# A fused attention and MLP block on one core: first loads split, W1's and Wkv's tails as steps of their own, all steps in a new order

## The chip, the cores and the metric

The kernel runs on one core of a Trainium2 chip. Its engines are TensorE (PE, with its weight loads as PEld), VectorE (DVE), ScalarE (ACT), GpSimd (POOL) and SyncE (SP); SP and ACT also issue the DMA transfers here, each on a queue of its own. The metric is the device time in microseconds (us). Before the change it is 150.41 us, the median of 3 runs (150.39 to 150.41).

## What is computed

The reference, cut to its core (bf16 inputs; S = 2048 tokens, D = 448, H = 16 heads of 28, F = 1792):

```python
xn = layernorm(x)                       # over D, eps 1e-5
q, k, v = split_heads(xn @ wqkv)
pq, pk = q @ w_phi, k @ w_phi           # per head, 28 x 28
phi_q = concat(softmax(pq), softmax(-pq))
phi_k = concat(softmax(pk), softmax(-pk))
kv, z = phi_k^T @ v, sum(phi_k)         # over the tokens
o = (phi_q @ kv) / (phi_q @ z + 1e-6)
h = xn @ w1 + b1
out = x + merge_heads(o) @ wo + (h * tanh(softplus(h))) @ w2
```

## The kernel before

The 2048 tokens are 16 tiles of 128 tokens; tile t holds every sixteenth token. Two tiles, 2u and 2u+1, form pair u; there are 8 pairs. The weights of q and k are multiplied with w_phi first (Wpq, Wpk), so that PE computes pq and pk directly. D = 448 is three chunks of 128 rows and a tail of 64; each tail is loaded twice, into either half of the 128 partitions, and the matmuls of a pair run two at a time on halves of 64 rows.

The program is recorded as named steps, and the string `ORDER` (L147 to L160) gives the order in which they are recorded. An engine runs its instructions in that order, so the string sets the order on PE, DVE, ACT, POOL and on the two DMA queues alike; waits on semaphores are put in from the data that each step reads and writes (`Program.op`, `resolve`). The banks of PSUM are also given out in that order: a step that needs a pair of banks takes the one that was given back longest ago (`take2`), and waits for whatever still reads it.

The steps of which the prediction speaks (a last letter names the engine or queue: s SP, a ACT, d DVE, p POOL, m the transposing DMA on SP):

- `lx..`: load of tiles of x (L269). `lkm`, `lvm`: the 384 main rows of Wk, Wv (L272). `lkt`: the tails of Wk and Wv in one (they are neighbours in memory), two DMAs (L279). `l1m0` to `l1m2`, `l1t`: W1's three chunks and its two tails. `lqT0` to `lqT3`: Wq, transposed by the DMA (L284); `qd` then copies 64 rows inside it on DVE (L288). `lp`: w_phi. `lb`: b1.
- `st6d`: mean and variance of tile 6, two rows on DVE (L467, L468), or three on ACT (`st3a`, L459 to L463). `rs3`: one over the standard deviation of pair 3, on ACT (L480, L482) or POOL (L473, L476). `xn3`: the normalised pair 3, three rows on DVE (L501), or a small shift on DVE (L489) and three rows on POOL (L496).
- `xt3`: the transposed pair 3, by seven PE transposes (L509) and a copy out of PSUM (L514 or L516), or by a DMA (L521).
- `z12`: 12 matmuls on constants at the start (L376). `wtk0` to `wtk3`: a chunk of Wk transposed on PE (wtr, L556) and copied out; `wmk0`.., `wmq0`..: a chunk of Wpk or Wpq, four matmuls with w_phi (wmm, L571) and a copy out. `b1`: a transpose on PE and a copy.
- `v31`, `v32`, `k31`, `q31`: first part (8 matmuls) and second part (6) of v, pk and pq for pair 3, all on L438. The second part is followed by the copy (L514, L516) or by two exponentials on ACT (L600 for k, L661 for q).
- `kn3.0`: half of phi_k's normalisation for pair 3: two rows on DVE (L608, L610) and a scaling on POOL (L612). `kv3`: the pair's part of kv (L629). `kvz`: kv out of PSUM, and a DMA transpose. `e4`: DMA transpose of tile 4's exponentials of q (L669).
- `f0.11`: first part of ffn1 for 128 features and half of the tokens (L438, 512 columns; ACT's Mish at L680 follows the second). `nd4`: numerator and denominator of tile 4 (L703), and DVE's seven rows on them. `ot2`: transpose of pair 2's o. `wo`, `G`, `g`: the matmuls with Wo and W2 (L843, L821, L805) and, with the last of a tile, the add on DVE (L770). `sto`: store of a pair.

Pair 3 is the first pair to be worked on, then pair 1; both are transposed on PE. Pair 2 is the first one transposed by the DMA.

Of the kernel before, what the change touches and what calls it, by code (L numbers as in the profile page):

```python
# [144 lines left out]


ORDER = """  # L147
lpa pp2 lx3s pm z12 st6d pi lkms table st7d pw lx1a lkts lba lvma bd rs3t wtk2a xn3d lx2s lqT2 wtk0d st3d pv wtk1a wmk2a
xt3a wtk3d lqT1 wmk0a wmk1a st2d wmk3a st5d v31d rs1p lqT0 st4d xn1d rs2p lqT3 b1 qd lx6s v32a k31 lx0s wmq1a lx4s pp1
wmq0a xn2p l1ts xt1d st14d st15d wmq2a wmq3a k32 k11 st12d rs7p st9d q11 xt2m st8d k12 st10d xn7d q31 rs4p v11d pp0 q12  # L150
xn4p st11d v12d q21 rs5p st13d q32 q22 xn5p k21 st0d l1m2s l1m0s rs6p xt7m v21d k22 st1d v22a ep e3 rs0p v71a pk xt4m
k71 v72a kn3.1 xn6d k72 xt5m k41 xn0d kn3.0 e2 xt6m xt0m v41d e5 k42 l1m1s v42d e4 q41 v51d q42 e6 e8 v52a kn2.0 k61
v61d k62 kn4.0 k01 k51 kn7.0 kn4.1 k02 v62d q51 k52 q52 kn0.0 e7 q61 e9 v01d q62 e12 kn1.1 kn6.1 e10 f0.11 e11 kn1.0
v02d f0.12 kn0.1 f1.01 f0.21 f1.02 f1.21 kn7.1 f1.31 f1.22 los kn2.1 q71 f1.32 f1.51 kn5.0 f0.22 e13 f1.52 q01 q72 q02
f0.61 l2s kn6.0 kv3 kv1 e15 kv2 kn5.1 kv4 kv6 e14 kv7 kv0 kv5 kvz f0.62 f0.71 f0.91 f1.81 f0.72 e1 f1.82 f0.121 f1.111
f0.122 f0.81 f0.92 f1.112 f0.82 f1.91 f0.131 f1.92 e0 nd2 f0.132 f0.31 f0.101 f0.32 nd0 f0.111 f0.102 f0.112 nd1 f1.71
f1.61 f1.72 f0.51 nd3 f1.62 f0.52 f1.41 f1.11 f0.01 f1.12 f0.41 f1.42 ot0m nd5 f0.42 f0.02 wo01 f1.131 f1.101 ot1m nd6
f1.132 G01 nd4 f1.102 G11 ot2m wob nd7 ot3m G02 wo02 f1.121 nd12 G12 f1.122 wo11 nd11 wo22 G31 wo31 nd10 wo12 G21 nd13
ot5m ot6m wo21 wo32 G62 nd8 G22 wo52 G32 nd9 ot4m wo61 G51 nd15 G61 nd14 wo51 G41 wo62 sto6 sto1 wo41 G52 ot7m g14 sto5
wo7F sto2 G42 wo7H sto0 wo42 g15 stt14 sto3 sto4 stt15  # L160
"""


# [5 lines left out]
def _kernel(es, nc, A_x, A_wqkv, A_w_phi, A_wo, B_w1, B_b1, B_w2, out):  # L169
    def sb(name, shape, dtype):  # L170
        return es.enter_context(nc.sbuf_tensor(name, shape, dtype))

# [103 lines left out]
    def load_chunk(eng, name, dst, src, c):  # L276
        dma(eng, lambda e: e.dma_start(dst[:, c, :], src[c * P:(c + 1) * P, :]), w=[(name, 0, c)], tag=f"ld{name}.{c}")
# [272 lines left out]
    def w_tr(c, eng):  # L550
        b = take1()
        to = bank16(b)[0:GP, 0:G * P].rearrange("p (g n) -> p g n", g=G)

        def tr(e):
            for g in range(G):
                ins = e.transpose(to[:, g, :], Wk[:, c, g * GP:(g + 1) * GP], ident[:])  # L556
# [431 lines left out]
```

## Time and profile before

| | |
|---|---|
| time, 3 runs | 150.39 to 150.41 us, median 150.41 |
| the profiled execution's own time | 150.35 us |
| its span, from the first to the last instruction | 148.3 us |
| granted TensorE clock | 0.999 |
| PE busy | 143.7 us (97%) |
| DVE busy | 100.7 us (68%) |
| ACT busy | 72.0 us (49%) |
| POOL busy | 44.4 us (30%) |
| share of the chain that ended last | PE 89%, DMA 6%, DVE 2% |

The profile is of one execution. A row of the timeline gives the start in us from the span's start, the busy time of a group of instructions that follow each other, the engine (or SPq, ACTq for the issuing of DMAs), the line, the operation, what it writes and reads by the program's tile names, the number of instructions, and in brackets how long the engine sat idle before it and what ended that. A matmul's own duration overlaps that of the next one, so the price of a matmul is read from start to start. A row of the chain of work that ended last gives start, length and the work. A row of the DMA issues ends with the time from issue to landing (the median, if there are several). In the tile names, Eq is also the home of the transposed Wk, and W stands for W1 or W2.

### The profile page before, as it was taken

The numbers are of one execution on the slowest core, as the hardware profiler recorded it, in microseconds if no ns is written. First come the engines' busy times: TensorE is split into PE (matmuls) and PEld (weight loads), VectorE is DVE, ScalarE is ACT, GpSimd is POOL, SyncE is SP. The second block draws the span as 40 slices with busy tenths as digits, with TensorE's granted clock in tenths as the row PEclk, the third lists the DMA queues.
The fourth block names the chain that finished last, engine by engine and source line by source line (L and its number), as shares of the span: only waits on it lengthen the run. The fifth ranks groups of instructions, "written<-read, shape, count | busy, mean of one in ns | idle before, by whom it ended". The sixth has DMA issues, their size and how long they took to land.

```text
span 148.3 us, 3988 instructions
## 1 busy us (share of the span) xinstructions
PE 143.7 (97%) x1731; PEld 75.9 (51%) x1731; DVE 100.7 (68%) x225; ACT 72.0 (49%) x83; POOL 44.4 (30%) x65
## 2 busy tenths in 40 slices
PE   7799999999999999999999999999999999999993
PEld 2456456556555475444454445555555555554452
DVE  0888889897999803003998278896789859983042
ACT  3589889978996899578566653202000000000000
POOL 5428489899899990000000000000000000000000
PEclk9999999999999999999999999999999999999999
DMA  5999998999939989960003300031003300306513
GB/s 123 301 190 346 182 275 130 163 205 256 139 67 174 242 242 267 210 113 0 0 4 62 62 4 0 21 73 34 4 2 66 62 0 4 62 4 186 186 52 134
DMA packets 39997, 17.24 MB, mean 116 GB/s; under 512 B 33964, under 2 KB 39212, under 8 KB 39980
## 3 DMA queue, kind: packets, MB, share of 16 engines
q1 hardware_dynamic: 38800, 16.29, 52.5%
q10 hardware_dynamic: 1180, 0.70, 1.9%
q8 instruction: 13, 0.21, 0.6%
q14 instruction: 4, 0.03, 0.1%
HBM read 7.02 MB, written 1.84 MB: 60 GB/s over the span
## 4 chain that ended last, share of the span: by engine, by line
PE 89%; DMA 6%; DVE 2%; issue 0%; ACT 0%; SPq 0%
PE PS L438 47%; PE PS L843 31%; PE PS L805 3%; DMA Wkv<-in_A_wqkv_dram 3%; DMA xnT<-xn 3%; PE PS L703 2%; PE PS L629 2%; PE PS L571 1%; PE PS L821 1%; DVE stats L467 1%; PE PS L556 1%; PE PS L509 1%; DVE xnT L516 0%; ACT Eq L514 0%; DVE x_all L770 0%
## 5 line engine op out<-in xcount | busy, mean ns | idle before, releaser
L438 PE MATMUL PS<-xnT,W 64*128 64x512 bf16 x392 | 44.8, 376 | 0.0
L680 ACT ACTIVATE actT<-PS,b1T 128x1024 bf16<-128x1024 f32 x28 | 30.1, 1112 | 24.3 <-PE PS L438 24.3
L843 PE MATMUL PS<-W,actT 64*128 64x448 bf16 x392 | 39.3, 349 | 0.0
L438 PEld LDWEIGHTS PS<-xnT,W 64*128 64x128 bf16 x392 | 18.8, 94 | 20.8 <-ACT actT L680 0.5
L843 PEld LDWEIGHTS PS<-W,actT 64*128 64x128 bf16 x392 | 18.1, 94 | 18.1 <-issue 0.3
L612 POOL TENSOR_TENSOR actT<-actT,rSk 128x896 bf16<-128x896 bf16 x16 | 26.6, 1702 | 0.7 <-DVE rSk L610 0.6
L770 DVE TENSOR_TENSOR x_all<-PS,x_all 128x448 bf16<-128x448 f32 (+1 forms) x16 | 9.2, 616 | 11.3 <-PE PS L821 5.6
L718 DVE COPY Sq<-PS 128x16 f32<-128x16 f32 x32 | 4.1, 169 | 18.6 <-PE PS L703 18.5
L608 DVE TENSOR_REDUCE Sk<-actT 128x32 f32<-128x896 bf16 x16 | 16.7, 1043 | 0.0
L600 ACT ACTIVATE actT<-PS 128x896 bf16<-128x896 f32 x16 | 13.8, 950 | 1.0 <-PE PS L438 0.9
L438 PE MATMUL PS<-Wkv,xnT 64*128 64x448 bf16 x112 | 13.2, 349 | 0.0
L438 PE MATMUL PS<-Wpq,xnT 64*128 64x448 bf16 x112 | 12.5, 349 | 0.4 <-DMA xnT<-xn 0.4
L467 DVE BATCH_NORM_STATS2 stats<-x_all 128x6 f32<-128x448 bf16 x16 | 9.7, 608 | 4.1 <-DMA x_all<-in_A_x_dram 4.1
L438 PE MATMUL PS<-Wpk,xnT 64*128 64x448 bf16 x112 | 12.5, 349 | 0.0
L726 DVE TENSOR_TENSOR v_all<-v_all 128x464 f32<-128x464 f32 x16 | 10.3, 642 | 0.6
L722 DVE TENSOR_TENSOR v_all<-PS,Sq 128x464 f32<-128x464 f32 x16 | 10.3, 642 | 0.5
L729 DVE TENSOR_TENSOR xn<-v_all,rden 128x448 bf16<-128x448 f32 x16 | 10.0, 625 | 0.6
L724 DVE TENSOR_TENSOR v_all<-PS,Sq 128x464 f32<-128x464 f32 x16 | 10.1, 631 | 0.0
L661 ACT ACTIVATE actT<-PS 128x896 bf16<-128x896 f32 x10 | 8.6, 921 | 1.1 <-PE PS L438 1.1
L438 PEld LDWEIGHTS PS<-Wpq,xnT 64*128 64x128 bf16 x112 | 5.9, 94 | 5.4 <-issue 0.8
L438 PEld LDWEIGHTS PS<-Wpk,xnT 64*128 64x128 bf16 x112 | 6.0, 94 | 4.4
L438 PEld LDWEIGHTS PS<-Wkv,xnT 64*128 64x128 bf16 x112 | 6.0, 94 | 4.3
(82 smaller groups left out, 126.4 us busy)
## 6 DMA issues: line engine op xcount, KB each, us to landing
W<-in_B_w_dram SPq DMA_DIRECT2D x1, 1568.0 KB, 10.1
out_dram<-x_all SPq DMA_DIRECT2D x7, 224.0 KB, 2.1
W<-in_B_w_dram SPq DMA_DIRECT2D x3, 448.0 KB, 4.1
x_all<-in_A_x_dram SPq DMA_DIRECT2D x2, 448.0 KB, 4.9
x_all<-in_A_x_dram SPq DMA_DIRECT2D x3, 224.0 KB, 3.8
Wo<-in_A_wo_dram SPq DMA_DIRECT2D x2, 336.0 KB, 4.1
W<-in_B_w_dram SPq DMA_DIRECT2D x2, 224.0 KB, 6.4
Wkv<-in_A_wqkv_dram SPq DMA_DIRECT2D x1, 336.0 KB, 4.5
```

What stands on the lines that cost most here:

```text
L438: ins = e.matmul(o, lhs(c, k), rhs(c, k), start=part == "1" and c == 0, stop=part == "2" and c == 2)
L467: op("DVE", lambda e: e.bn_stats(stats[:, t, :], x_all[:, t, :]), r=[("x", t)], w=[("st", t)], tag=f"bn{t}")
L600: op("ACT", lambda e, s=s: e.activation(E_of(u)[:, s, :, :], two(b, D), ACT.Exp, scale=1.0 if s == 0 else -1.0), r=[pb(b), pb(b + 1)], w=[ ...
L608: op("DVE", lambda e: e.tensor_reduce(Sk[u][:, s, :], Eh(), AX.X, ALU.add), r=[("E", u, s)], w=[("Sk", u, s)], tag=f"Sk{u}.{s}")
L612: op("POOL", lambda e: e.tensor_tensor(Eh(), Eh(), ap_on(rSk[u][:, s, 0:1], [[1, 2 * H], [0, DH]]), ALU.mult), r=[("E", u, s), ("rSk", u, ...
L680: op("ACT", lambda e: e.activation(actT[:, fc, q * 1024:(q + 1) * 1024], bank(b, 2), ACT.Mish, bias=b1T[:, fc:fc + 1]), r=[("b1T",), pb(b) ...
L722: op("DVE", lambda e: e.tensor_tensor(tv(t1[i]), num(0), sx(1), ALU.mult), r=[pb(b), pb(b + 1), ("Sq", i, 1)], w=[("t1", i)], tag=f"ta{t}")
L724: op("DVE", lambda e: e.tensor_tensor(tv(t2), num(1), sx(0), ALU.mult), r=[pb(b), pb(b + 1), ("Sq", i, 0)], w=[("t2",)], tag=f"tb{t}")
L726: op("DVE", lambda e: e.tensor_tensor(t1[i], t1[i], t2, ALU.add), r=[("t1", i), ("t2",)], w=[("t1", i)], tag=f"tc{t}")
L729: op("DVE", lambda e: e.tensor_tensor(o_sb[(t // 2) % 2][:, t % 2, :].rearrange("p (h d) -> p h d", d=DH), t1[i][:, :, 0:DH], ap_on(rden[i ...
L770: op("DVE", lambda e: e.tensor_tensor(x_all[:, t, 0:n], bank(b)[:, 0:n], x_all[:, t, 0:n], ALU.add), r=[pb(b), ("x", t)], w=[("out", t)], ...
L843: ins = e.matmul(bank(places[par][0])[:, 0:D], l, r, start=fresh[par], stop=places[par][2] and i >= len(todo) - 2)
```

## The change

1. The first pair of x (tiles 6 and 7) is loaded as two loads of one tile each, on ACT's queue, in place of one load on SP's. (The load of pair 3 as a whole is no longer a step.)
2. The 384 main rows of Wk are loaded as three loads of 128 rows, each with a resource of its own, so that the transpose of a chunk waits for that chunk alone.
3. The two tails of Wk and Wv, and the two of W1, are four steps (`ly0`, `ly1`, `lz0`, `lz1`) in place of two, each on either queue.
4. All steps stand in a new order: which queue a load is on, which engine does a copy or a statistic, and the order itself. There are 14 warm matmuls in place of 12, and `mask2` and the clearing of KVT stand earlier on POOL.

No matmul of the computation is added or left out.

```diff
 ORDER = """
-lpa pp2 lx3s pm z12 st6d pi lkms table st7d pw lx1a lkts lba lvma bd rs3t wtk2a xn3d lx2s lqT2 wtk0d st3d pv wtk1a wmk2a
+pw pi lt6a lps lt7a pm bd lx1s st6d lk0a lba lk2a pv table st7d st2d lk1a ly0s ly1s lvma lx0a rs3a pp1 z14 lx2s xn3d
...
-    home_rows = {"Wk": [("Wk", 0), ("Wt", 0), ("Wt", 1)], "Wv": [("Wv", 0)], "Wq": [("WqT", g) for g in range(G)] + [("WqTd",)],
+    home_rows = {"Wk": [("Wk", 0, c) for c in range(3)] + [("Wt", 0), ("Wt", 1)], "Wv": [("Wv", 0)], "Wq": [("WqT", g) for g in range(G)] + [("WqTd",)],
...
-    def load_tail(eng, name, dst, src):
-        for i, (lo, hi) in enumerate(HALF):
-            dma(eng, lambda e, lo=lo, hi=hi: e.dma_start(dst[lo:hi, 3, :], src[384:448, :]),
-                w=[("Wt", i) if name == "Wkv" else (name, 1 + i)], tag="ld" + name)
+    def load_tail(eng, name, dst, src, i):
+        lo, hi = HALF[i]
+        dma(eng, lambda e: e.dma_start(dst[lo:hi, 3, :], src[384:448, :]), w=[("Wt", i) if name == "Wkv" else (name, 1 + i)],
+            tag="ld" + name)
...
-        pe(tr, rows_of("Wk")[:1 if c < 3 else 3] + [("ident",)], [pb(b)], f"wtr{c}")
+        pe(tr, ([("Wk", 0, c)] if c < 3 else [("Wt", 0), ("Wt", 1)]) + [("ident",)], [pb(b)], f"wtr{c}")
...
-        for name, a, b in (("x0", 0, 2), ("x1", 2, 4), ("x2", 4, 6), ("x3", 6, 8), ("x4", 8, 12), ("x6", 12, 16)):
+        for name, a, b in (("x0", 0, 2), ("x1", 2, 4), ("x2", 4, 6), ("t6", 6, 7), ("t7", 7, 8), ("x4", 8, 12), ("x6", 12, 16)):
             add(f"l{name}{c}", load_x, a, b, eng)
-        for i, (n, t) in enumerate((("k", Wk), ("v", Wv))):
-            add(f"l{n}m{c}", load_main, eng, "W" + n, t, A_wqkv[:, (i + 1) * D:(i + 2) * D])
-        add(f"lkt{c}", load_tail, eng, "Wkv", Wkv, A_wqkv[:, D:3 * D])
+        for i in range(3):
+            add(f"lk{i}{c}", load_chunk, eng, "Wk", Wk, A_wqkv[:, D:2 * D], i)
+        add(f"lvm{c}", load_main, eng, "Wv", Wv, A_wqkv[:, 2 * D:3 * D])
+        for i in range(2):
+            add(f"ly{i}{c}", load_tail, eng, "Wkv", Wkv, A_wqkv[:, D:3 * D], i)
+            add(f"lz{i}{c}", load_tail, eng, "W1", W1, B_w1, i)
         for i in range(3):
             add(f"l1m{i}{c}", load_chunk, eng, "W1", W1, B_w1, i)
-        add(f"l1t{c}", load_tail, eng, "W1", W1, B_w1)
```

Three places show the new order.

On **PE**, from the end of the setup to the first matmul on pair 2. Wpk rows are k, Wpq rows q, Wkv rows v. Before; the last row holds q21 (8, the first of pair 2), q32 and q22:

```order
L438 MATMUL PS<-Wpk,xnT 128x448 x14
L438 MATMUL PS<-Wpq,xnT 128x448 x8
L438 MATMUL PS<-Wpk,xnT 128x448 x6
L438 MATMUL PS<-Wpq,xnT 128x448 x8
L438 MATMUL PS<-Wkv,xnT 128x448 x8
L438 MATMUL PS<-Wpq,xnT 128x448 x6
L438 MATMUL PS<-Wkv,xnT 128x448 x6
L438 MATMUL PS<-Wpq,xnT 128x448 x20
```

The change, at the same place; the last row is v21, the first of pair 2:

```order
L438 MATMUL PS<-Wpk,xnT 128x448 x14
L438 MATMUL PS<-Wpq,xnT 128x448 x8
L438 MATMUL PS<-Wpk,xnT 128x448 x6
L438 MATMUL PS<-Wpq,xnT 128x448 x6
L438 MATMUL PS<-Wkv,xnT 128x448 x8
L438 MATMUL PS<-Wpq,xnT 128x448 x8
L438 MATMUL PS<-Wkv,xnT 128x448 x6
L438 MATMUL PS<-Wpq,xnT 128x448 x6
L438 MATMUL PS<-Wkv,xnT 128x448 x8
```

In both, the first row is k32 and k11, and ahead of it stand v3 (14) and k31 (8). The second part of q3 (q32, 6 matmuls) has moved ahead of the first matmul on pair 2, and that one is of v, no longer of q.

On **DVE**, the start of the program. Before (L467 and L468 are tiles 6, 7; then xn3; then the copy of wtr0; then tile 3):

```order
L467 BN_STATS stats<-x_all 128x6
L468 BN_AGGR mv<-stats 128x2
L467 BN_STATS stats<-x_all 128x6
L468 BN_AGGR mv<-stats 128x2
L501 TENSOR_SCALAR xn<-x_all,mv,rstd 128x448
L501 TENSOR_SCALAR xn<-x_all,mv,rstd 128x64
L501 TENSOR_SCALAR xn<-x_all,mv,rstd 128x384
L516 COPY Eq<-PS 112x512
L467 BN_STATS stats<-x_all 128x6
```

The change, from tile 7 on (then tile 2, xn3, and the copies of wtr0, b1, wtr1, xT3):

```order
L467 BN_STATS stats<-x_all 128x6
L468 BN_AGGR mv<-stats 128x2
L467 BN_STATS stats<-x_all 128x6
L468 BN_AGGR mv<-stats 128x2
L501 TENSOR_SCALAR xn<-x_all,mv,rstd 128x448
L501 TENSOR_SCALAR xn<-x_all,mv,rstd 128x64
L501 TENSOR_SCALAR xn<-x_all,mv,rstd 128x384
L516 COPY Eq<-PS 112x512
L516 CAST b1T<-PS 128x14
L516 COPY Eq<-PS 112x512
L516 COPY xnT<-PS 128x896
```

Tile 2's statistics now stand ahead of xn3; tile 3's are gone from DVE (ACT has them); the copy of xT3 has come from ACT to DVE. Behind these rows come the copy of wtr3 and xn1.

On **SP**'s queue, W1's tails. Before, behind the loads of x (the transposing DMA of L521 is pair 2's):

```order
L270 DMA x_all<-in_A_x_dram 128x1792
L281 DMA W<-in_B_w_dram 64x1792 x2
L521 DMA_TRANSPOSE xnT<-xn 128x7x128
L277 DMA W<-in_B_w_dram 128x1792 x2
L521 DMA_TRANSPOSE xnT<-xn 128x7x128
```

The change, right behind the transposing DMA of pair 0 (the L521 row here is pair 5's):

```order
L281 DMA W<-in_B_w_dram 64x1792
L669 DMA_TRANSPOSE EqT<-Eq 128x8x128
L521 DMA_TRANSPOSE xnT<-xn 128x7x128
L277 DMA W<-in_B_w_dram 128x1792
L669 DMA_TRANSPOSE EqT<-actT 128x8x128 x2
L669 DMA_TRANSPOSE EqT<-Eq 128x8x128
L281 DMA W<-in_B_w_dram 64x1792
```

The two tails stood together ahead of pair 2's transposing DMA, where now one of W1's chunks stands; they are now apart, the first behind five pairs' transposing DMAs, the second behind the last chunk and three transposes of q.

More of the change, by code (lines that the diff above doesn't have):

```diff
@@ L147 @@
 ORDER = """
-lpa pp2 lx3s pm z12 st6d pi lkms table st7d pw lx1a lkts lba lvma bd rs3t wtk2a xn3d lx2s lqT2 wtk0d st3d pv wtk1a wmk2a
[L149 to L157, printed above, removed]
@@ L158 @@
-f1.132 G01 nd4 f1.102 G11 ot2m wob nd7 ot3m G02 wo02 f1.121 nd12 G12 f1.122 wo11 nd11 wo22 G31 wo31 nd10 wo12 G21 nd13
-ot5m ot6m wo21 wo32 G62 nd8 G22 wo52 G32 nd9 ot4m wo61 G51 nd15 G61 nd14 wo51 G41 wo62 sto6 sto1 wo41 G52 ot7m g14 sto5
-wo7F sto2 G42 wo7H sto0 wo42 g15 stt14 sto3 sto4 stt15
+pw pi lt6a lps lt7a pm bd lx1s st6d lk0a lba lk2a pv table st7d st2d lk1a ly0s ly1s lvma lx0a rs3a pp1 z14 lx2s xn3d
+st3a wtk0d b1 lqT1 lqT0 lqT3 wtk2a wtk1d lqT2 rs1a xt3d wmk0a lx6s wtk3d wmk1a wmk2a v31d xn1d wmk3a st5d xt1a st4d rs2a
@@ new lines @@
+qd v32a k31 st1d pk xn2p wmq2d wmq1d lx4s wmq0a st14d l1m2s wmq3a k32 pp0 st15d rs7p st8d k11 ep q11 k12 q12 st9d xn7d
+st0d rs4p v11a xt2m xn4p q31 v12d rs0p st13d q32 v21d st12d rs6p st10d l1m0s pp2 xt7m k21 v22a q21 k22 e3 q22 v71a xt4m
+xn6d st11d xn0d e2 rs5a k71 v72d xt6m q41 k72 xn5p k41 v41a k42 kn1.1 kn2.1 v42d k61 kn7.0 q42 kn7.1 k62 xt0m kn4.0 v61d
+lz1s k01 v62a k02 e7 xt5m kn4.1 v51d l1m1s q51 kn6.1 v52d e5 e4 q52 k51 v01a e6 k52 kn6.0 kn5.0 v02a kn2.0 q61 lz0s
+f1.31 q62 f1.32 f1.01 f0.11 kn3.0 e9 e8 e12 e11 f0.21 f1.02 e10 f0.22 f0.12 f1.51 kn5.1 e13 q71 kn3.1 f1.21 q01 f1.52
@@ new lines @@
+f1.22 q02 q72 f1.91 kv4 kn0.1 kv2 kv5 kv3 kn0.0 los kv7 kv6 kn1.0 kv0 kv1 kvz f1.61 f1.92 f1.71 f1.62 f0.111 f1.72 e0
+f0.61 f1.101 f0.62 f1.102 e15 f1.131 nd3 f0.112 f1.132 f0.131 f0.71 f0.101 f0.132 e1 nd1 f0.72 e14 f0.102 f0.01 f0.31
+nd2 f0.02 l2s f1.111 f0.32 f1.112 f0.81 nd0 f0.121 f0.82 f0.41 f0.122 ot1m nd7 f0.51 f0.42 f0.91 f0.52 f0.92 nd6 ot0m
+f1.11 f1.121 wo11 nd4 f1.122 ot3m G11 f1.12 nd5 G02 nd10 nd11 wo01 G12 G01 ot2m nd13 G31 ot5m wo02 nd14 wo12 wo31 f1.41
+wo32 nd15 ot7m G32 f1.81 f1.42 G21 wob f1.82 nd12 wo51 ot6m wo21 wo52 G62 wo22 sto0 nd9 sto1 G22 G61 sto2 nd8 ot4m wo61
@@ L161 @@
+G51 wo7F sto3 g14 G52 wo41 wo7H G41 sto5 wo62 G42 wo42 sto6 sto4 stt14 g15 stt15
 """
@@ L292, in rows_of @@
     def rows_of(name):
-        if name in ("Wk", "Wv"):
+        if name == "Wv":
             return [(name, 0), ("Wt", 0), ("Wt", 1)]
```

## The prediction

> **What bounds the kernel now.** First the chain of work that ended last, in order of time, then the busy time by stretch (span of the stretch, then PE, PE's weight loads, DVE, ACT, POOL, the granted clock, the DMA share, GB/s).
>
> ```profile
> 1.26 4.54 DMA Wkv<-in_A_wqkv_dram
> ...
> 14.22 4.29 DMA xnT<-xn
> ...
> 18.64 34.54 PE PS L438 x350
> 53.19 3.27 PE PS L629 x128
> ...
> 5.94:18.64 12.70, 11.85 (x141) 7.05 (x142) 10.73 (x34) 10.78 (x18) 5.92 (x13) 1.00 1.03 248
> 18.64:53.19 34.55, 34.55 (x353) 19.30 (x354) 30.44 (x57) 30.56 (x34) 32.63 (x34) 1.00 1.01 178
> 53.19:145.40 92.21, 92.21 (x1218) 47.63 (x1219) 56.69 (x130) 28.33 (x28) 2.35 (x4) 1.00 0.31 71
> ```
>
> From 18.64 to 145.40 PE is busy without a gap, at full granted clock: the chain there is PE's own work, and both kernels have the same matmuls. What an order can win lies ahead of 18.64, where the chain runs through loads, DVE and, last, the transposed load of pair 2 (issued at 14.22, landed 4.29 later). So two questions decide: how much of PE's work is done when PE has to stop for pair 2, and when pair 2 comes.
>
> **The term that counts.** It needs the price of a matmul:
>
> ```profile
> 15.44 0.92 PE L438 MATMUL PS<-Wpq,xnT 64*128 64x448 bf16 x8
> ...
> 16.19 0.92 PE L438 MATMUL PS<-Wkv,xnT 64*128 64x448 bf16 x8
> ...
> 18.64 2.07 PE L438 MATMUL PS<-Wpq,xnT 64*128 64x448 bf16 x20 [0.40 <-DMA xnT<-xn]
> ```
>
> From start to start 8 take 0.75 us, 0.094 each; with the gaps between groups (350 in 34.54, some of them of 512 columns) I use 0.095. The PE rows shown with the change give the count ahead of the wait: before, 8 + 14 for k31 and v3, then 14 + 8 + 6 + 8 + 8 + 6 + 6 = 56, so 78; after, 22 and then 14 + 8 + 6 + 6 + 8 + 8 + 6 + 6 = 62, so 84 (q32 now stands ahead of the wait). If PE resumes at 18.64 again, 6 x 0.095 = **0.57 us** less work is left behind it.
>
> **Whether PE is there by 18.64.** Rows of the start, and two landing times:
>
> ```profile
> 0.85 4.65 PE L376 MATMUL PS<-const-bfloat16-1.0 128*128 128x512 bf16 x12 [0.85 <-PEq L973]
> ...
> 1.30 0.48 ACTq L270 DMA_DIRECT2D x_all<-in_A_x_dram  x1
> ...
> 2.50 0.41 ACTq L273 DMA_DIRECT2D Wkv<-in_A_wqkv_dram  x1
> ...
> 4.40 0.59 DVE L467 BATCH_NORM_STATS2 stats<-x_all 128x6 f32<-128x448 bf16 x1
> ...
> 5.17 1.23 DVE L501 TENSOR_SCALAR xn<-x_all,mv,rstd 128x448 bf16<-128x448 bf16 x3
> ...
> 8.28 0.42 DVE L516 COPY Eq<-PS 112x512 bf16<-112x512 bf16 x1 [0.50 <-PE PS L556]
> 8.62 0.62 DVE L467 BATCH_NORM_STATS2 stats<-x_all 128x6 f32<-128x448 bf16 x1
> ...
> 9.37 0.59 DVE L467 BATCH_NORM_STATS2 stats<-x_all 128x6 f32<-128x448 bf16 x1
> ...
> 10.83 0.86 DVE L501 TENSOR_SCALAR xn<-x_all,mv,rstd 128x448 bf16<-128x448 bf16 x3
> ...
> 11.49 0.57 PE L571 MATMUL PS<-Wbd,WqT 112*128 112x112 bf16 x8
> 11.60 0.17 DVE L516 CAST b1T<-PS 128x14 f32<-128x14 bf16 x1
> ...
> 11.68 0.22 DVE L289 COPY WqT<-WqT 128x256 bf16<-128x256 bf16 x1
> ...
> 11.89 0.56 PE L509 MATMUL PS<-ident,xn 128*128 128x128 bf16 x7
> ...
> 12.49 0.62 DVE L516 COPY xnT<-PS 128x896 bf16<-128x896 bf16 x1
> ...
> 13.03 0.62 DVE L467 BATCH_NORM_STATS2 stats<-x_all 128x6 f32<-128x448 bf16 x1
> ...
> Wkv<-in_A_wqkv_dram ACTq DMA_DIRECT2D x1, 336.0 KB, 5.2
> x_all<-in_A_x_dram ACTq DMA_DIRECT2D x1, 224.0 KB, 4.1
> ```
>
> DVE's new order puts tile 2's statistics, which wait for pair 1, ahead of xn3. Queued behind that wait are xn3, the copies of wtr0, b1, wtr1, xT3 and wtr3, and xn1: all that PE needs next. Pair 1 keeps its place behind the w_phi load, on SP's queue instead of ACT's, so I put it where it was, 1.30 + 4.1 = 5.40. From statistics to xn is 0.77 (4.40 to 5.17); xn lets DVE go on after 0.77 (10.83 to 11.60) and is done after 0.86; a 112x512 copy takes DVE 0.34, b1's 0.08, an xnT copy 0.54. So xn3 runs from 6.17 to 7.03, wtr0's copy from 6.94, b1's from 7.28, wtr1's from 7.36, xT3's from 7.70 to 8.32, wtr3's from 8.24, xn1 from 8.58 to 9.44.
>
> PE: xT3 goes at 7.1. What stands ahead of it is done by then: Wk's three parts follow the halves of x3 as Wk followed x3, 1.26 + 4.54 = 5.80, so the splits of x and Wk are worth nothing here by themselves; the two more warm matmuls, at 4.65/12 each, end by 6.3, and 12 wtr matmuls and b1 after them by 7.0; ACT's eight issues (0.41 to 0.48 each) end by 5.2, ahead of its first computation. Then 0.40 for xT3 and 0.05 for each wmm or wtr matmul (8 from 11.49 to 11.89): v31 at 8.4, wmm13 9.2, xT1 at 9.5 behind xn1, v32 9.9, k31 10.5, the four steps wmm0 11.25, k32 12.05, k11 12.6, q11 13.4. The 48 matmuls from q11 to q32 take 4.56: PE is ready for pair 2 at **18.0**, 0.6 early.
>
> That margin has to cover what the trace doesn't show. ACT's mean and square of tile 3 (two rows of 448 columns and a tiny one) cost between nothing and three times the 0.92 of an 896-column copy, quoted below; I take 1.2, nearest to the 0.46 of a 448-column copy, which ends ahead of 7 and is hidden until wtr2's copy is wanted at 8.2. Wv landed at 2.50 + 5.2 = 7.70, that is 2.30 after pair 1, on ACT's queue. Now x3's and Wk's 560 KB go ahead of it there, as they went on SP's queue: 5.80 + 2.30 = 8.1, against v31 at 8.4.
>
> **When pair 2 comes.** Its xn2 runs on POOL, behind one small row of DVE and a root of ACT:
>
> ```profile
> 4.61 0.29 ACT L480 ACTIVATE lnv<-mv,eps_col 128x1 f32<-128x1 f32 x1 [2.06 <-DVE mv L468]
> ...
> 10.84 0.92 ACT L514 ACTIVATE v_all<-PS 128x896 bf16<-128x896 f32 x1 [0.67 <-PE PS L438]
> ...
> 11.90 1.85 ACT L514 ACTIVATE Wpq<-PS 128x448 bf16<-128x448 f32 x4
> ...
> 12.18 0.16 DVE L489 SCALAR_TENSOR_TENSOR shift<-mv,rstd 128x2 f32<-128x2 f32 x1 [0.27 <-POOL rstd L476]
> ...
> 12.45 1.74 POOL L496 TENSOR_SCALAR xn<-x_all,rstd,shift 128x448 bf16<-128x448 bf16 x3
> ```
>
> After xn1 DVE is free at 9.35; three tiles' statistics at 0.75 (8.62 to 9.37) and the copy inside WqT bring the shift to 11.8. If that copy still has to wait until 11.68, its time in the trace, the shift comes at 12.6. Shift to issue took 14.22 - 12.18 = 2.04, so the issue falls between 13.8 and 14.6, and with the old 4.29 the landing between 18.1 and 18.9. Ahead of it SP's queue carries 448 KB of W1 in either kernel (one chunk in place of two tails), and the DMA share of 1.03 says that the transfers queue. I take 18.51 as before, so PE at 18.64. ACT has from 10.1 on the copies of xT1 and v3 (0.92 each), a root (two rows of 0.3) and two copies into Wpq (0.46 each): done by 13.4, so q11 stands.
>
> **Sum.** The profiled execution took 150.35 us with its span of 148.3, beside a median of 150.41. 150.35 - 0.57 = **149.8**. Ends of the same case: pair 2 early and PE at 18.0 gives 0.57 + 0.64 = 1.2 less, 149.15; pair 2 at 18.9 leaves 0.2, 150.15.
>
> **Rivals.**
>
> ```profile
> L770 DVE TENSOR_TENSOR x_all<-PS,x_all 128x448 bf16<-128x448 f32 (+1 forms) x16 | 9.2, 616 | 11.3 <-PE PS L821 5.6
> L726 DVE TENSOR_TENSOR v_all<-v_all 128x464 f32<-128x464 f32 x16 | 10.3, 642 | 0.6
> ...
> 30.82 0.58 SPq L277 DMA_DIRECT2D W<-in_B_w_dram  x1
> ...
> 34.69 1.32 SPq L669 DMA_TRANSPOSE EqT<-actT  x1
> ...
> 38.62 16.61 POOL L612 TENSOR_TENSOR actT<-actT,rSk 128x896 bf16<-128x896 bf16 x10 [0.64 <-DVE rSk L610]
> ...
> 39.83 1.04 PE L438 MATMUL PS<-xnT,W 64*128 64x512 bf16 x8
> ...
> W<-in_B_w_dram SPq DMA_DIRECT2D x1, 448.0 KB, 3.9
> W<-in_B_w_dram SPq DMA_DIRECT2D x2, 224.0 KB, 6.4
> ```
>
> 1. *The lead is used up on the way (no change, 150.1 to 150.5).* Two places are tight. The phi_k scalings ended at 38.62 + 16.61 = 55.23; the last kv step starts at 53.19 + 7/8 x 3.27 = 56.05. Of these 0.82 the lead takes 0.57, and POOL's first scaling now stands behind xn5, which waits for ACT and DVE in turn: a stream 0.8 later than before costs the whole lead. And where nd13, nd14 and nd15 follow each other, DVE has per nd four rows of some 0.64 and small ones, about 3 us, and two adds of 0.62 between, while PE brings 62 matmuls, 5.9 us, from nd13 to nd15: about half a microsecond to spare, by my count. For this rival: ACT and DVE are 88% busy until kv (30.56 and 30.44 of 34.55). Against: PE waited nowhere there. Chance 0.22.
>
> 2. *W1's last tail comes late (slower).* It moved from ahead of pair 2 to behind the last W1 chunk and three EqT transposes on SP. Those took 34.69 + 1.32 - 30.82 = 5.2, and the chunk's issue should fall between 29.7 and its old 30.82: the tail goes out between 34.9 and 36.0. The first ffn1 matmul wants it at 39.83 - 0.57 = 39.26, with all of PE queued behind. With the chunk's 3.9 it lands between 38.8 and 39.9; with the tails' own 6.4, at 41.3 or later. A landing after 39.83 makes the kernel slower: at 41.0 it takes 150.35 + 1.17 = 151.5. Against: the 6.4 was measured behind 1120 KB of x, and here only transposes stand ahead. Chance 0.14.
>
> 3. *Wv is late (slower if past 9.6).* The margin takes it until 9.0, and at 9.6 the gain is gone. At ACT's old pace from the start (588 KB by 7.70, 76 KB per us) the 900 KB that Wv now ends would have landed at 11.8: 150.35 + 2.2 = 152.6. Chance 0.08.
>
> The Trainium skill bears on the third. Its page DMA: Bandwidth & Descriptors, section Queues, rings and completion order, says that a DMA engine serves the queues in turn, a packet at a time. By that rule ACT's queue has its turns whatever SP holds, Wv is not later than 8.1, and the sum stays. The trace agrees for Wv's own stretch (336 KB in the 2.30 us after pair 1, beside SP's tails) and not for the time before it, when SP landed 560 KB by 5.80 and ACT 248 KB by 5.40.
>
> That the splits bring nothing is part of the forecast already; the order alone would then give the same.
>
> **How the numbers follow.** Forecast 149.8, chance 0.56. A measurement of this kernel can tell 0.2%, 0.3 us, from no change: faster 0.56, same 0.22, slower 0.22. The range, 149.2 to 150.9, takes in the early pair 2, the no-change case, and of the two slower ones a delay of 1.1 us (the tail landing at 40.4); beyond it lie about two in ten.
>
> **What would show it.** Right: xT3 at about 7.1, q11 near 13.4, v21 waiting for the transposed load and going between 18.0 and 18.7, the first ffn1 matmul near 39.3, kv near 52.6, no PE wait after 18.7. Wrong: q11 after 14.1, PE waiting for W1 or behind POOL's scaling, or v21 going late without a wait for pair 2.

## The result and the profile after

The changed kernel is **slower**: 152.44 us (median of six) beside 150.4, a ratio of 1.0129 with a 95% interval of 1.0095 to 1.0164. Ratios are of fast runs alone, so one of these six, of 154.63, counts in the median and not in the ratio; the other five lie between 151.44 and 152.91. The forecast was 149.8, the range 149.2 to 150.9. The profiled run is the fastest of the new kernel's, 151.44 us with a span of 149.7 (before: 150.35 and 148.3), at full granted clock.

The chain of waits of the new kernel, in order of time (start, length, work), then its busy time by stretch, columns as before:

```profile
2.29 0.68 ACTq L302
...
3.43 4.95 DMA Wkv<-in_A_wqkv_dram
...
14.07 26.59 PE PS L438 x280
40.66 0.56 issue
41.22 13.32 PE PS L438 x126
54.54 3.27 PE PS L629 x128
```

```profile
5.66:19.87 14.21, 12.41 (x147) 7.51 (x149) 13.12 (x43) 12.41 (x26) 5.41 (x14) 1.00 0.92 242
19.87:41.22 21.35, 20.79 (x220) 10.54 (x217) 18.94 (x35) 18.18 (x24) 17.15 (x19) 1.00 1.05 183
...
54.54:146.70 92.16, 92.16 (x1216) 49.05 (x1217) 56.70 (x129) 29.19 (x28) 2.06 (x4) 1.00 0.31 71
```

From kv on both kernels take the same (92.16 here, 92.21 before), so all of the loss lies ahead of it: kv begins at 54.54 in place of 53.19. It comes in two pieces. The first is ahead of 19.87, where the chain no longer runs through pair 2's transposed load but through the last part of Wk, issued at 3.43. The second is a hole of 0.56 us at 40.66, where PE had no gap before. The timeline of PE shows both:

```profile
7.30 0.43 PE L556 MATMUL PS<-ident,Wkv 128*112 128x128 bf16 x4 [1.06 <-DMA Wkv<-in_A_wqkv_dram]
8.43 0.43 PE L556 MATMUL PS<-ident,Wkv 128*112 128x128 bf16 x4 [0.69 <-DMA Wkv<-in_A_wqkv_dram]
8.69 0.55 PE L509 MATMUL PS<-ident,xn 128*128 128x128 bf16 x7
...
10.12 0.93 PE L438 MATMUL PS<-Wkv,xnT 64*128 64x448 bf16 x8
...
15.33 0.92 PE L438 MATMUL PS<-Wpq,xnT 64*128 64x448 bf16 x8
...
19.87 0.92 PE L438 MATMUL PS<-Wkv,xnT 64*128 64x448 bf16 x8
...
41.22 1.04 PE L438 MATMUL PS<-xnT,W 64*128 64x512 bf16 x8 [0.56 <-ACT actT L661]
```

xT3 (8.69) stands behind the third transpose of Wk and goes 1.6 us later than forecast (7.1); q11 at 15.33 instead of 13.4; the first matmul on pair 2 at 19.87, with no wait for pair 2. Those were signs named for a wrong forecast. The landings, each asked for by the moment of its issue (0.82 and 1.27 for the halves of x, 1.80, 2.99 and 3.43 for Wk's chunks 0, 2 and 1, 15.42 for pair 2's transpose, 36.58 for W1's last tail; the last column is the time from issue to landing):

```profile
x_all<-in_A_x_dram ACTq DMA_DIRECT2D x1, 112.0 KB, 2.4
x_all<-in_A_x_dram ACTq DMA_DIRECT2D x1, 112.0 KB, 3.9
Wkv<-in_A_wqkv_dram ACTq DMA_DIRECT2D x1, 112.0 KB, 3.7
Wkv<-in_A_wqkv_dram ACTq DMA_DIRECT2D x1, 112.0 KB, 4.3
Wkv<-in_A_wqkv_dram ACTq DMA_DIRECT2D x1, 112.0 KB, 5.0
xnT<-xn SPq DMA_TRANSPOSE x1, 3.0
W<-in_B_w_dram SPq DMA_DIRECT2D x1, 224.0 KB, 4.5
```

So the halves of x landed at 3.2 and 5.2 (the whole, before, at 0.81 + 2.8 = 3.6), Wk's parts at 5.5, 7.3 and 8.4 (the whole at 5.8). W1's last tail landed at 36.58 + 4.5 = 41.1; the profile names the exponentials of q5 (L661) for the hole, but they ended at 38.87 + 1.73 = 40.6, and PE went on 0.14 us after the tail. And pair 2's transposed load, which the forecast left at 4.29, took 3.0.

### The profile page after: what moved, and what is told of

Its sections match the earlier page's. It is cut to its first block, busy times and chain, and to the rows that moved or that the text cites. A ratio compares the mean times of both kernels' runs of the same rounds, so it can differ in the third digit from the quotient of the medians.

```text
span 149.7 us, 3997 instructions
## 1 busy us (share of the span) xinstructions
PE 143.7 (96%) x1733; PEld 76.2 (51%) x1733; DVE 101.4 (68%) x226; ACT 72.5 (48%) x89; POOL 41.4 (28%) x59
## 3 DMA queue, kind: packets, MB, share of 16 engines
q10 hardware_dynamic: 1436, 1.25, 3.2%
## 4 chain that ended last, share of the span: by engine, by line
PE 92%; DMA 3%; ACTq 2%; issue 1%; DVE 1%; ACT 0%
PE PS L438 50%; PE PS L843 31%; PE PS L805 3%; DMA Wkv<-in_A_wqkv_dram 3%; PE PS L703 2%; PE PS L629 2%; PE PS L571 1%; PE PS L821 1%; ACTq L270 1%; ACTq L277 1%; PE PS L509 1%; ACTq L302 0%; PE PS L556 0%; DVE x_all L770 0%; DVE x_all L791 0%
## 5 line engine op out<-in xcount | busy, mean ns | idle before, releaser
L438 PE MATMUL PS<-xnT,W 64*128 64x512 bf16 x392 | 45.2, 376 | 0.6 <-ACT actT L661 0.6
L438 PEld LDWEIGHTS PS<-xnT,W 64*128 64x128 bf16 x392 | 19.1, 94 | 21.1 <-ACT actT L661 1.0
L843 PEld LDWEIGHTS PS<-W,actT 64*128 64x128 bf16 x392 | 19.2, 94 | 17.1 <-issue 0.4
L438 PE MATMUL PS<-Wkv,xnT 64*128 64x448 bf16 x112 | 13.2, 349 | 0.1
L438 PE MATMUL PS<-Wpq,xnT 64*128 64x448 bf16 x112 | 13.1, 349 | 0.0
L438 PE MATMUL PS<-Wpk,xnT 64*128 64x448 bf16 x112 | 12.9, 349 | 0.0
L467 DVE BATCH_NORM_STATS2 stats<-x_all 128x6 f32<-128x448 bf16 x15 | 9.1, 610 | 4.3 <-DMA x_all<-in_A_x_dram 4.3
L661 ACT ACTIVATE actT<-PS 128x896 bf16<-128x896 f32 x10 | 8.7, 923 | 1.8 <-DMA EqT<-actT 1.7
L438 PEld LDWEIGHTS PS<-Wpq,xnT 64*128 64x128 bf16 x112 | 5.7, 94 | 5.1
L496 POOL TENSOR_SCALAR xn<-x_all,rstd,shift 128x448 bf16<-128x448 bf16 (+2 forms) x9 | 5.2, 594 | 11.1 <-DVE shift L489 11.1
L438 PEld LDWEIGHTS PS<-Wpk,xnT 64*128 64x128 bf16 x112 | 5.4, 94 | 5.0
```

Of the source, the lines that this page charges most:

```text
L438: ins = e.matmul(o, lhs(c, k), rhs(c, k), start=part == "1" and c == 0, stop=part == "2" and c == 2)
L467: op("DVE", lambda e: e.bn_stats(stats[:, t, :], x_all[:, t, :]), r=[("x", t)], w=[("st", t)], tag=f"bn{t}")
L843: ins = e.matmul(bank(places[par][0])[:, 0:D], l, r, start=fresh[par], stop=places[par][2] and i >= len(todo) - 2)
```

## The experiments

Eleven altered kernels and the change once more, in three groups on two chips, each timed against the kernel before on the same chip (its medians there are 150.34 to 150.49). "Pair 2" is the start of the first matmul on pair 2 in the profiled run, "hole" PE's idle time ahead of the first ffn1 matmul. Both are of one execution each. In the edits of `ORDER` only the steps that differ and their neighbours are shown; "..." stands for steps left out.

| kernel | median us | ratio to before, 95% | profiled run us | pair 2 | hole |
|---|---|---|---|---|---|
| before | 150.4 | 1 | 150.35 | 18.64 | none |
| the change | 152.44 | 1.0129 (1.0095 to 1.0164) | 151.44 | 19.87 | 0.56 |
| after_again | 153.38 | 1.0176 (1.0128 to 1.0223) | 154.05 | 21.90 | 0.88 |
| a_w1tails_early | 151.90 | 1.0080 (1.0046 to 1.0115) | 152.49 | 20.43 | 0.31 |
| a_queues | 152.55 | 1.0117 (1.0064 to 1.0170) | 152.53 | 20.09 | 1.53 |
| a_first_loads_of_before | 151.07 | 1.0026 (0.9995 to 1.0057) | 151.19 | 18.82 | 1.34 |
| a_wk_whole | 151.78 | 1.0087 (1.0057 to 1.0117) | 151.60 | 19.25 | 1.33 |
| a_whole_act | 150.94 | 1.0035 (1.0007 to 1.0063) | 150.31 | 18.34 | 0.91 |
| b_wk_split | 151.66 | 1.0083 (1.0058 to 1.0108) | 151.59 | 19.65 | none |
| b_tails_late | 151.87 | 1.0094 (1.0061 to 1.0127) | 151.84 | 18.40 | 0.36 |
| c_start_and_tails | 150.28 | 0.9991 (0.9962 to 1.0020) | 150.26 | 19.36 | none |
| c_start_tails_turns | 150.07 | 0.9978 (0.9957 to 0.9999) | 150.47 | 19.61 | none |
| d_tails_behind_pair2 | 150.33 | 1.0002 (0.9977 to 1.0028) | 149.90 | 18.34 | none |
| a_kept_warm | 152.24 | 1.0108 (1.0075 to 1.0141) | 152.32 | 20.50 | 0.67 |

### The first loads: queue or split

**a_queues**, the queues of the first loads exchanged, splits kept:

```diff
-lt6a lps lt7a ... lx1s ... lk0a ... lk2a ... lk1a
+lt6s lpa lt7s ... lx1a ... lk0s ... lk2s ... lk1s
```

> The changed kernel with the queues of its first loads exchanged: both halves of pair 3's x and Wk's three parts on SP, w_phi and pair 1 on ACT; the splits and the order stay. Theory A (the queue decides, ACT's lands its rows late): the half with tile 7 lands near 4 instead of 5.1 us, Wk's last part by 6.5 instead of 8.4, the first matmul on pair 2 at 18.7 to 19.2 instead of 19.87; time 0.6 to 1.1 us less. Theory B (the splits decide, on whichever queue: more and smaller transfers, each some 4 us from its issue, which stand one behind the other): tile 7 at about 5, Wk's last part at 7.5 or later, the first matmul on pair 2 at 19.5 or later; time within 0.4 us of the changed kernel's.

Theory B. Wk's three parts went out on SP at 1.73, 2.2 and 2.67; the last column is the time to landing:

```profile
Wkv<-in_A_wqkv_dram SPq DMA_DIRECT2D x1, 112.0 KB, 3.6
...
Wkv<-in_A_wqkv_dram SPq DMA_DIRECT2D x1, 112.0 KB, 4.5
...
Wkv<-in_A_wqkv_dram SPq DMA_DIRECT2D x1, 112.0 KB, 5.6
```

They landed at 5.3, 6.7 and 8.25, pair 2 began at 20.09, and the time did not fall. The queue is not it. Nor is it the moment of issue: the last part went out 0.76 us earlier than in the change (3.43) and landed only 0.1 earlier.

**a_first_loads_of_before**, pair 3 of x and Wk whole and on SP again (w_phi and pair 1 on ACT), the order and all else as changed:

```diff
-lt6a lps lt7a ... lx1s ... lk0a ... lk2a ... lk1a
+lx3s lpa ... lx1a ... lkms
```

> The changed kernel with the first loads as before: pair 3 of x whole and Wk whole on SP, w_phi and pair 1 on ACT; order and all else as changed. Theory A (the first loads are what was lost at the start, and the order is worth what was predicted): Wk lands near 5.8, q11 at 13.4 to 14.0, the first matmul on pair 2 waits for its transposed load and goes at 18.0 to 18.9; time 1.0 to 1.6 us less than the changed kernel's, that is 0.1 to 0.6 us above the kernel before because of the wait ahead of the first ffn1 matmul. Theory B (the new order of DVE's and PE's steps at the start is late by itself): Wk lands near 5.8 and the first matmul on pair 2 still goes at 19.5 or later; time within 0.4 us of the changed kernel's.

Theory A in the main: pair 2 at 18.82, 1.05 us earlier, and a median 1.4 us below the change's. The new order of DVE and PE is not late by itself. But PE did not wait for pair 2's load, which had landed at 14.44 + 3.0 = 17.4: it was late on its own account (q11 at 14.28, where 13.4 to 14.0 was expected), and the hole ahead of ffn1 grew to 1.34, so that this profiled run is only 0.25 us shorter than the change's.

**a_wk_whole**, only Wk whole again, where its first part stood on ACT:

```diff
-lt6a ... lt7a ... lk0a ... lk2a ... lk1a
+lt6a ... lt7a ... lkma
```

> The changed kernel with Wk's 384 rows in one load at the place of its first part, still on ACT's queue and behind the two halves of pair 3's x. Theory A (the split of Wk is what is late: three loads of 128 rows land one after the other 1.1 to 1.7 us apart, wherever they are issued, as the kernel with the queues exchanged showed with 5.3, 6.7 and 8.25): the whole lands 4.4 to 4.9 after its issue at 1.80, that is at 6.2 to 6.8, and the first matmul on pair 2 goes at 18.6 to 19.3; time 0.6 to 1.3 us less than the changed kernel's. Theory B (the place on ACT's queue is what is late): it lands at 7.5 or later, and the first matmul on pair 2 stays at 19.6 or later.

Wk landed at 1.79 + 5.3 = 7.1, between the two theories' times, but pair 2 began at 19.25 and the median is 0.7 us below the first runs of the change and 1.6 below after_again: theory A.

**a_whole_act**, x whole too; against the kernel just above, x in one load or in two is the only difference:

```diff
-lt6a ... lt7a ... lk0a ... lk2a ... lk1a
+lx3a ... lkma
```

> The changed kernel with pair 3's x in one load and Wk in one load, but on ACT's queue where the change has them, and w_phi and pair 1 on SP: only the queues of the first loads differ from the kernel with the first loads of before (151.07, first matmul on pair 2 at 18.82). Theory A (the splits are all that is late): x lands near 3.7, Wk near 5.8, the first matmul on pair 2 goes at 18.7 to 19.0, time within 0.3 us of 151.07. Theory B (ACT's queue is late by itself): Wk at 6.5 or later, the first matmul on pair 2 at 19.2 or later, time 0.4 us or more above 151.07.

Theory A by the time (150.94), with pair 2 even earlier than it said; Wk landed at 1.26 + 4.9 = 6.2, between the two theories' times. Its timeline of PE (line numbers are 4 higher here, L442 for L438):

```profile
7.23 0.56 PE L513 MATMUL PS<-ident,xn 128*128 128x128 bf16 x7
...
8.54 0.93 PE L442 MATMUL PS<-Wkv,xnT 64*128 64x448 bf16 x8
...
13.80 0.92 PE L442 MATMUL PS<-Wpq,xnT 64*128 64x448 bf16 x8
...
18.34 0.92 PE L442 MATMUL PS<-Wkv,xnT 64*128 64x448 bf16 x8
```

xT3 at 7.23, v3 at 8.54, q11 at 13.80, pair 2 at 18.34, without a wait: this is the forecast's start (7.1, 8.4, 13.4, 18.0 ready), with both loads on ACT's queue. From 19.87 to 18.34 the profiled runs give 0.62 to the split of Wk (19.87 to 19.25) and 0.91 to that of x (19.25 to 18.34). The split of x works through Wk: behind two loads of x Wk went out at 1.79 and took 5.3, behind one at 1.26 and took 4.9. The shares are rough, since they come from one execution each and the changed kernel itself gave 19.87 and, in after_again, 21.90.

**b_wk_split**, the kernel before with Wk's split alone:

```diff
-lpa pp2 lx3s pm z12 st6d pi lkms table
+lpa pp2 lx3s pm z12 st6d pi lk2s lk0s lk1s table
```

> The kernel before with nothing changed but Wk's 384 rows in three loads on SP (chunks 2, 0, 1, in the order in which PE wants them). Theory A (the split itself is slow): the three land near 5.0, 6.3 and 7.8 us, in place of 5.7 for the whole; PE, which waited 0.40 us for pair 2, has 1.0 to 2.0 us less time, so the time rises by 0.5 to 1.5 us. Theory B (the split costs nothing on SP's queue, as the prediction said): the last lands by 6.3, the time stays within 0.3 us of the kernel before.

Theory A: +1.3 us (151.66 beside 150.34). Its parts went out at 1.27, 1.7 and 2.2:

```profile
Wkv<-in_A_wqkv_dram SPq DMA_DIRECT2D x1, 112.0 KB, 3.0
...
Wkv<-in_A_wqkv_dram SPq DMA_DIRECT2D x1, 112.0 KB, 4.0
...
Wkv<-in_A_wqkv_dram SPq DMA_DIRECT2D x1, 112.0 KB, 4.8
```

So they were issued some 0.45 us apart and landed 1.3 to 1.4 apart, at 4.3, 5.7 and 7.0. The timeline of PE shows that only part of the price is paid there:

```profile
7.08 0.43 PE L556 MATMUL PS<-ident,Wkv 128*112 128x128 bf16 x4 [0.92 <-DMA Wkv<-in_A_wqkv_dram]
...
9.46 0.93 PE L438 MATMUL PS<-Wkv,xnT 64*128 64x448 bf16 x8
...
19.65 2.07 PE L438 MATMUL PS<-Wpq,xnT 64*128 64x448 bf16 x20 [1.00 <-DMA xnT<-xn]
```

v3 goes 0.40 later than before (9.06), and pair 2 1.0 later: it was issued at 14.60 instead of 14.22 and took 4.9 instead of 4.3. Why it took longer is not shown.

### The hole ahead of ffn1

**a_w1tails_early**:

```diff
-l1m2s wmq3a
+l1m2s lz0s lz1s wmq3a
...
-v61d lz1s k01
+v61d k01
...
-q61 lz0s f1.31
+q61 f1.31
```

> The changed kernel with both tails of W1 right behind W1's chunk 2 on SP's queue (issue near 10.4 and 11.0 us, when SP has nothing to do until 15.4). Theory A (PE's 0.56 us ahead of the first ffn1 matmul is W1's last tail, issued at 36.58 and landed 4.5 later at 41.1): the wait goes but for some 0.1 us, since the exponentials of q5 end at 40.60 and PE is free at 40.66; time 0.4 to 0.5 us less than the changed kernel's. Theory B (the wait is the exponentials of q5, L661, as the profile names it, and they are late because of the transposes of tiles 4 and 5): these transposes are issued some 0.6 to 1.7 us earlier only as far as a tail stood ahead of them; the wait stays between 0.3 and 0.6. Under either theory the start stays: Wk's last part at about 8.4, first matmul on pair 2 at about 19.9.

The hole shrank to 0.31, at the lower end of theory B, in a run that was late from the start (Wk's last part at 9.0). The median is 0.5 us below the change's and 1.5 below that of after_again, which ran beside it; the intervals of change and repair overlap, so the size of the gain is not settled. The rows of ACT and PE show who is next:

```profile
39.74 1.73 ACT L661 ACTIVATE actT<-PS 128x896 bf16<-128x896 f32 x2 [1.98 <-DMA EqT<-actT]
```

```profile
41.52 1.04 PE L438 MATMUL PS<-xnT,W 64*128 64x512 bf16 x8 [0.31 <-ACT actT L661]
```

Here PE does go on when L661 ends (39.74 + 1.73 = 41.47), and L661 itself waited for the transposes of tiles 4 and 5, which the new order puts behind more of SP's queue. In the seven profiled runs that have a late tail (the change and six of these runs, all with the new order) PE went on 0.04 to 0.14 us after the tail landed and 0.5 to 0.8 after L661 had ended. So both theories are right, one behind the other: the tail holds PE in those seven, and L661 is next.

**b_tails_late**, the kernel before with only W1's tails moved:

```diff
-xn2p l1ts xt1d
+xn2p xt1d
...
-e6 e8
+e6 l1ts e8
```

> The kernel before with nothing changed but W1's two tails moved behind tile 6's transpose on SP, about where the change has its second one. Theory A (the tails' place is a loss of its own, by the prediction's second rival): they go out near 35.5 to 37.0 and land at 40.5 to 41.3, PE, which wants them at 39.8 or earlier, waits 0.7 to 1.5 us; pair 2's transposed load comes up to 1.3 us earlier and gives 0.2 to 0.4 back, since PE waited 0.40 for it; time 0.3 to 1.1 us above the kernel before. Theory B (they are hidden): no wait there, time at or up to 0.4 us below the kernel before.

Theory A, but dearer: +1.4 us. Its timeline of PE has two holes:

```profile
40.11 1.04 PE L438 MATMUL PS<-xnT,W 64*128 64x512 bf16 x8 [0.36 <-DMA W<-in_B_w_dram]
...
44.20 4.11 PE L438 MATMUL PS<-xnT,W 64*128 64x512 bf16 x36 [0.97 <-ACT Eq L661]
```

The first is the tail (issued at 35.80, landed 4.2 later at 40.0). The second is what the tails pushed back on SP: tile 7's transpose, issued at 38.78 and landed 3.6 later at 42.4, goes before the exponentials into Eq, which begin at 42.42, and PE waits for the banks that these read. (The profile names PE's own matmuls for ACT's wait here; that it is the transpose is read from the 0.04 us between its landing and their start.)

**c_start_and_tails**, the two repairs together (the edits of a_first_loads_of_before and a_w1tails_early):

> The changed kernel with the first loads of the kernel before and with W1's tails right behind W1's chunk 2 on SP. If the two losses are separate and add up: first matmul on pair 2 near 18.8 as with the first loads alone; the wait ahead of the first ffn1 matmul, 1.34 us there, shrinks to between 0.1 and 0.8, since the exponentials of q5 wait for the transposes of tiles 4 and 5, which go out some 0.6 us earlier than the 31.1 to 35.0 there; time 0.5 to 1.2 us less than with the first loads alone (151.07), that is 149.9 to 150.6. If the tails don't matter when the start is right: within 0.3 us of 151.07.

They add up: no hole, 150.28, the time of the kernel before. Pair 2 began at 19.36, not near 18.8 as expected: PE reached it only at 19.18, having waited 0.35 us for xn3 ahead of xT3 (7.91), and its load, now behind the tails, landed no sooner (14.63 + 4.6 = 19.2).

**c_start_tails_turns**, with the transposes of tiles 4 and 5 around pair 5's as well:

```diff
-e7 xt5m kn4.1 v51d l1m1s q51 kn6.1 v52d e5 e4 q52
+e5 xt5m e4 kn4.1 v51d l1m1s e7 q51 kn6.1 v52d q52
```

> As the kernel with the first loads of before and early tails, and with the transposes of tiles 4 and 5 on either side of pair 5's transposing load instead of behind it, W1's last chunk and tile 7's. If the exponentials of q5 are what is left of the wait ahead of the first ffn1 matmul: they start by 37.0, the wait is gone (PE goes on at about 39.6), and the time is 149.6 to 150.2, at or below the kernel before. If pair 5 or another wait takes its place (v5 is wanted at about 33.4 us), PE waits there instead and the time stays within 0.3 us of the kernel with early tails alone.

150.07, a ratio of 0.9978 (0.9957 to 0.9999): the lowest median of all. A gain on the kernel before is not shown by that: the interval all but touches 1, this is the best of eleven kernels, and the interval of c_start_and_tails, where the hole was gone already, overlaps it. In its profiled run PE lost 0.80 us again, to pair 2's transposed load. The chain of waits:

```profile
14.27 5.21 DMA xnT<-xn
...
19.61 33.94 PE PS L442 x344
```

That load took 4.1 to 5.2 us in the four of these kernels with W1's two tails ahead of it (4.3 in the kernel before), and 2.9 to 3.4 in the change, both times, and in the seven kernels without them there.

**d_tails_behind_pair2**, the tails behind it:

```diff
-l1m2s lz0s lz1s wmq3a
+l1m2s wmq3a
...
-l1m0s pp2
+l1m0s lz0s lz1s pp2
```

> As the last kernel (first loads of before, transposes of tiles 4 and 5 around pair 5's), with W1's two tails behind W1's chunk 0, so behind pair 2's transposing load instead of ahead of it. Pair 2's load took 3.0 us from issue to landing where no W1 tail stood ahead of it and 4.3 to 5.2 where two did. If that is the tails' doing, it lands about 3.0 after its issue near 14.3, PE doesn't wait for it (first matmul on pair 2 at 18.5 to 18.9 with 84 matmuls done), and with no wait ahead of the first ffn1 matmul the time is 149.3 to 149.9, 0.4 to 1.0 us below the kernel before. If it is not, the load takes 4 us or more again and the time stays within 0.3 us of 150.07.

Half a miss. Pair 2 took 3.0 and PE began it at 18.34 without a wait, and the profiled run is the shortest of all (149.90). But the median stayed at 150.33, and PE waits once more, six us on:

```profile
25.08 0.93 PE L442 MATMUL PS<-Wpq,xnT 64*128 64x448 bf16 x8 [0.52 <-DMA xnT<-xn]
```

This is pair 4's transposed load, issued at 20.26 and landed 4.7 later, now that the tails stand ahead of it. The tails' price goes to the transposes behind them: in c_start_tails_turns the same load took 4.1, and pair 7's, which is the first behind the tails here, took 4.8 instead of 3.8.

### The spread of the changed kernel

> The changed kernel once more, nothing altered, for its spread: its runs so far lie between 151.4 and 152.9 us, while those of the kernel before lie within 0.4 us. Theory A (the lateness is made by the first loads): a run that takes longer than the profiled 151.44 shows its Wk parts or a half of x landing later than 8.4 and 5.1 us, and the first matmul on pair 2 later than 19.87, by the same amount. Theory B (the rest is lost elsewhere): the first matmul on pair 2 stays within 0.1 us of 19.87 and a longer run has a second PE wait behind it longer than the 0.56 us ahead of the first ffn1 matmul.

The profiled run took 154.05. Its busy time by stretch (PE, weight loads, DVE, ACT, POOL, granted clock) and the v3 row of PE:

```profile
7.30:9.25 1.95, 0.70 (x9) 0.56 (x10) 0.66 (x4) 1.65 (x6) 0.12 (x1) 1.00 1.01 220
9.25:12.50 3.25, 3.25 (x32) 2.48 (x32) 2.72 (x7) 1.52 (x3) 0.00 (x0) 0.53 1.25 286
```

```profile
11.48 1.60 PE L438 MATMUL PS<-Wkv,xnT 64*128 64x448 bf16 x8
```

Wk's last part landed at 8.9 instead of 8.4, as theory A has it, but pair 2 began 2.0 us late, not 0.5: PE, which had stood idle for 0.39 and 1.25 us, was granted half its clock for some 3 us behind that, and 8 matmuls took 1.60 instead of 0.93. Theory B's part is the 0.88 ahead of ffn1.

**a_kept_warm**, matmuls on constants in those gaps:

```diff
-wtk0d b1 lqT1
+wtk0d b1 z4 lqT1
...
-wtk2a wtk1d
+wtk2a z3 wtk1d
```

> The changed kernel with 4 more matmuls on constants ahead of the second, and 3 ahead of the third transpose of Wk, where PE stood idle for 1.06 and 0.69 us (1.25 in a slower run, in which the granted clock then fell to 0.50 for some 3 us and the first matmul on pair 2 went at 21.9). Theory A (the idle PE is what lets the clock fall, and this makes the changed kernel's runs spread over 1.5 us and more): the granted clock stays at 1.0, the runs lie within 0.8 us of each other or near the fastest of the changed kernel, median 151.3 to 152.0. Theory B (the spread is that of the loads' landing): the spread of over 1 us and the median of 152.4 to 153.4 stay.

Undecided. The clock stayed at 1.0 and the six runs lie between 151.43 and 152.32, so none is as slow as the slowest of the change; but the median, 152.24, hardly moved, and its pair 2 began at 20.50 behind a last part of Wk that landed at 9.1. So the typical loss is there without the clock, and the clock comes on top in some runs. How often can be read from the granted clock on record for each run: of the 30 runs of the three kernels with the change's five first loads and no added matmuls (the change, a_queues, a_w1tails_early), seven have a mean clock of 0.978 to 0.989, and they are the slowest of their kernel, from 153.25 up; of the 66 runs of the six kernels with the new order and Wk whole none has, of 68 of the kernel before two. But the change also reached 153.49 at 1.0, and six runs without such a one are too few to show that the added matmuls prevent it.

## Why the prediction was wrong

**The step that failed** is the sentence "Wk's three parts follow the halves of x3 as Wk followed x3, 1.26 + 4.54 = 5.80, so the splits of x and Wk are worth nothing here by themselves". It took a time for 560 KB and assumed that the same bytes in five loads need the same time. In the change they landed by 8.4, and on either queue each further part of Wk came 1.1 to 1.8 us after the one ahead (2.3 once, in a_kept_warm). a_queues excludes the queue, a_whole_act shows that x and Wk whole are back in time on ACT as well, and b_wk_split charges 1.3 us to one of the two splits in the old kernel. Why a part needs so long behind another is not shown. The Trainium skill, Perfetto Trace Analysis, section DMA Optimizations, says that splitting may let some transfers start sooner, and that where the DMA engines are generally idle it may let the whole task end sooner. The first holds here (the first part at 4.3 in b_wk_split, against 5.8 for the whole). The whole did not end sooner (the last part at 7.0), and the DMA engines were not idle: their share is 0.92 from 1.27 to 7.00 there.

**What that hid.** With whole loads on ACT's queue PE follows the forecast's times to within 0.4 us, so most of the first step stood. In a_first_loads_of_before, with both whole on SP's queue, PE is up to 0.9 us behind them without a wait for a load, and there a smaller term failed: "the two more warm matmuls, at 4.65/12 each, end by 6.3". The row of all 14 there:

```profile
0.85 6.12 PE L380 MATMUL PS<-const-bfloat16-1.0 128*128 128x512 bf16 x14 [0.85 <-PEq L980]
```

They ended at 6.97, and at 6.28 in a_whole_act, and xT3 went at 7.72 and 7.23. The 14 took 4.51 in the profiled run of the change, where PE then waited for Wk, and 4.98 to 6.12 in the ten others that have 14. Every repaired kernel kept the 14; whether 12 would have started PE sooner was not tried.

The term of the sum stood: 344 matmuls take 33.94 from pair 2 to kv in c_start_tails_turns, 350 took 34.54 before, so the six were worth 0.60 for the 0.57 forecast. Even so no repaired kernel has a median of 149.8: c_start_tails_turns lost 0.80 again to pair 2's load, d_tails_behind_pair2 0.52 to pair 4's.

**Pair 2** was not the bound that the forecast made of it. "I take 18.51 as before" used 4.29 for the load; behind one chunk of W1 instead of two tails it took 3.0. It was issued late (15.42 for 13.8 to 14.6, since DVE was) and still landed at 18.4, ahead of PE.

**Rival 2 came true**, at a chance of 0.14. SP's timeline (W1's last chunk, then the tail):

```profile
31.51 0.58 SPq L277 DMA_DIRECT2D W<-in_B_w_dram  x1
...
36.58 1.66 SPq L281 DMA_DIRECT2D W<-in_B_w_dram  x1
```

From the chunk to the tail it is 5.07 (5.2 forecast), but the chunk itself went out at 31.51, not between 29.7 and 30.82, because everything ahead of it was late. The tail landed at 41.1, past the 39.83 from which the rival decides. That is 0.56 us in the profile, and 1.4 us when both tails move there in the old kernel, with what this pushes back on SP. What the rival had missed is that second mechanism, the transposes that free the homes of the exponentials. Rival 3 came close to being seen: Wv landed at 3.88 + 6.1 = 10.0, past the 9.6 named there, but PE reached v3 at 10.12 behind Wk, so no more than 0.1 us is its own. Rival 1 did not appear; POOL kept up.

**The size.** In the profiled runs, pair 2 begins 19.87 - 18.64 = 1.23 later, the matmuls from there to kv take 54.54 - 19.87 - 0.56 = 34.11 instead of 34.55, 0.44 less, and the hole adds 0.56: the 1.35 by which kv is late. The median is another 1.0 above the profiled run, which was the new kernel's best. In the four profiled runs with these loads on these queues (the change, after_again, a_w1tails_early, a_kept_warm) Wk's last part landed at 8.4, 8.9, 9.0 and 9.1, which fits; that it makes up the 1.0 is not shown.

## What to carry to other kernels

A load that is split to let its first part be used early pays for each further part: here the last of three landed 1.2 us later than the whole in the old kernel and 1.3 in the new, so split only what nothing waits to see complete. A small load moved late in a queue is to be priced with the issue time of everything ahead of it and with its full latency, and with what it pushes back on its own queue. Where an order wins at one place, look at once at the next two waits, since a gain at the start is paid back at the first late transfer.
